# Gated linear attention followed by a ReGLU block: two tokens a partition in steps 0 and 1, one batch in each half of the partitions

## The chip, the cores and the metric

The kernel runs on one core of one Trainium2 chip. The metric is the device time of one execution in microseconds (us). Before the change it is 196.01 us, the median of three runs (194.18 to 196.87).

The engines go by the names of the profile: PE (TensorE, matmuls; PEld is its weight load), DVE (VectorE), ACT (ScalarE), POOL (GpSimd) and SP (SyncE, which here only issues DMAs). SPq and POOLq are the sequencers of SP and POOL at work on a DMA issue. L834 is line 834 of the kernel before.

## The reference

There are 4 batches, 8 heads, 768 tokens and a head dimension of 48. For each batch and head a state of 48 x 48 runs over the tokens, and its output goes through a feed-forward block with a ReLU gate:

```python
f = 1.0 / (1.0 + np.exp(-f_logit))
for t in range(S):
    state = f[:, :, t, :, None] * state + np.einsum('bhd,bhe->bhde', k[:, :, t], v[:, :, t])
    y[:, :, t] = np.einsum('bhd,bhde->bhe', q[:, :, t], state)
x = y.transpose(0, 2, 1, 3).reshape(B * S, H * D)       # 3072 x 384
out = (np.maximum(x @ w_gate, 0.0) * (x @ w_val)) @ w_out   # d_ff = 1536
```

## The kernel before, in words

**Tiling.** The 768 tokens are cut into six steps of C = 128 tokens. A step handles 128 tokens of all four batches; the batches go in two pairs (pair 0 is batches 0 and 1). Within a step the recurrence becomes matmuls. The logarithms of f are summed over the tokens by a matmul with a triangle of ones ("cum"). Their exponentials scale q and k to q-hat and k-hat ("hats"). Both are transposed, so that the head dimension lies in the partitions (qkT). Scores are k-hat times q-hat, masked to the triangle (ptm). x is scores times v plus q-hat times the old state. k-hat times v, added to the old state and scaled by the total decay, gives the new state. The feed-forward block follows: gate and val (L834, 12 slices of d_ff, three matmuls each), ReLU on ACT (L840), the product on DVE (L844), and the output matmuls (L877) with a copy on ACT (L887) and a store by SP (L891).

**Two ways for the attention.** Steps 1 to 5 have one token in each of the 128 partitions for f, k, q and v (`attention_front`, then `attention`): a load (L473) reads runs of 192 B, one for each token and head. Step 0 (`twos = (0,)`) has two tokens in a partition for f, k and q, so that its loads read runs of 384 B; its v is still loaded one token a partition. In step 0 partition 2r + b holds the tokens 2r and 2r + 1 of batch b of the pair. `attention_pair` computes the hats of a pair for both tokens i = 0 and 1, transposes them (L609) and copies k's transposes on DVE (L617) and q's on ACT (L616). `tokens` reads a batch's tokens from there in their natural order with a stride of two. Scores, rows and state of step 0 then run in `attention`, as in other steps. For step 0's state k-hat must stand with one token a partition, so `attention_back` transposes it back (L631, 4 matmuls a batch) and copies it on DVE (L636).

**Two ways for the transposes of the hats.** For (step, pair) in `pe_hats`, which are both pairs of steps 1 and 2, PE transposes (L694, 8 matmuls a batch) and DVE copies (L699). In steps 3 to 5 SP issues a transposing DMA, "the crossbar" (L702).

**Two ways for x.** "tiled" (steps 0 to 2): matmuls with 32 columns of weights, four tiles side by side in the array (L759), give x already transposed, which ACT copies to xT (L788). "xbar" (steps 3 to 5): full matmuls give x untransposed (L767, L771), ACT copies it (L793) and SP transposes it by DMA (L795).

**Scores** (L724) have 48 rows a head: even heads lie in the partitions from 0, odd ones from 64, and two run in the two halves of the array's rows. `s_twin` and `y_twin` name the pairs whose two batches' scores or rows are issued as one block.

**What sets the order.** The kernel contains a planner (`Plan`). Each instruction is added with an estimated time, a priority and the tiles that it reads and writes; a list scheduler with PSUM bank limits fixes the order of each engine's instructions and the semaphore waits. The order is then static: an engine that meets something that is not ready stands still, and all behind it waits. Loads go on SP's queue in the order of `first` and then step by step, at most `flight = 3` ahead; SP also issues the stores and the crossbar transposes, in one order. The weights (wg, wv, wo) are loaded by POOL's queue in three slices each; their issue waits for certain loads (`wg0@f0.1` means that wg's slice 0 waits until f of step 0, pair 1 has landed).

**The start.** While nothing else is ready, PE runs matmuls of zeros (L938).

Of the kernel before, what the change touches and what calls it, by code (L numbers as in the profile page):

```python
# [299 lines left out]
def bass_hgrn2_outer__then__ffn_reglu_kernel(  # L300
# [10 lines left out]
    twos = (0,)  # L311
    pe_hats = {(1, 0), (1, 1), (2, 0), (2, 1)}
    halves = {0: 6, 1: 6, 2: 6}
    x_way = {(c, pr): "tiled" if c < 3 else "xbar" for c in range(6) for pr in range(2)}
    s_twin = {(c, pr) for c in range(6) for pr in range(2)} - {(0, 0), (1, 0)}
    y_twin = {(1, 1), (2, 0), (2, 1)}
# [5 lines left out]
    C = 128  # L322
# [51 lines left out]
    pick2 = sb("pick2", [128, 2], BF16)  # L374
    ident = sb("ident", [128, 128], BF16)
# [4 lines left out]
    pl = Plan({"bc": 2, "bc4": 4, "tp": 2, "s": 4, "y": 2, "kv": 1, "f": 4})  # L380
# [28 lines left out]
    def triangle(t, name, base, prio):  # L409
# [9 lines left out]
                                         pattern=[[0, 64], [1, 2]], channel_multiplier=-1), ["pick"], ["pick"], occ=0.3, prio=-20)  # L419
# [10 lines left out]
    add("DVE", lambda: ve.tensor_copy(pick2[:], same.ap[:, 0:2]), [same], ["pick2"], occ=0.1, prio=-19)  # L430
# [30 lines left out]
    def load(n, c, b0, b1, after=()):  # L461
        last = tails.get("load")
        t = ld[n]
        both = c in twos and n != "v"
        if both:
            src = bass.AP(tensor=srcs[n].tensor, offset=b0 * H * S * D + c * C * D,
                          ap=[[2 * D, C // 2], [S * D, 2 * H], [1, 2 * D]])
            dst = bass.AP(tensor=t, offset=slot_of(n, c, b0 // 2) * 2 * HD, ap=[[NL[n] * 2 * HD, 128], [2 * D, H], [1, 2 * D]])
        else:
            src = bass.AP(tensor=srcs[n].tensor, offset=b0 * H * S * D + c * C * D,  # L470
                          ap=[[D, C], [S * D, (b1 - b0) * H], [1, D]])
            dst = t[:, slot_of(n, c, b0 // 2), :, :, :].rearrange("p b h d -> p (b h) d")
        op = add("SP", lambda: sy.dma_start(dst, src), [], in_keys(n, c, b0, b1),  # L473
                 occ=0.7 if both else 1.0, lat=0.9, prio=c * 100, after=after,
                 follows=[last] if last else [])
        tails["load"] = op
        dma(op, f"{n}{slot_of(n, c, b0 // 2)}", 0.95 * (b1 - b0), (64, 19, 27) if both else (128, 13.5, 23))
        return op
# [20 lines left out]
    loads, done = [], {}  # L499
    for item in first:  # L500
        item, _, behind = item.partition("@")
        gate = [done[behind]] if behind else []
        if item[0] == "w":
            op = load_w(item[:2], int(item[2:]), gate)
        else:
            c, pr = (int(x) for x in item[1:].split("."))
            op = load(item[0], c, 2 * pr, 2 * pr + 2, gate)
        done[item] = op
        if item[0] != "w":
            loads.append(op)  # L510

    def chain(line, *args, **kw):

        last = tails.get(line)
        tails[line] = add(*args, follows=[last] if last else [], **kw)
        return tails[line]
# [10 lines left out]
    def tokens(c, b, x, p, lo=0, hi=128):  # L527
        qi = (c * B + b) % NQ
        if c not in twos:
            return qkT[lo:hi, qi, x, p, :]  # L530
        row, two = NQ * 2 * NP * C, b % 2
        return bass.AP(tensor=qkT, offset=lo * row + (qi - two) * 2 * NP * C + x * 2 * NP * C + p * 2 * C + two,
                       ap=[[row, hi - lo], [2, C]])
# [18 lines left out]
    def attention_pair(c, b0):  # L552
# [3 lines left out]
        raw = {n: ld[n][:, slot_of(n, c, pr), :, :, :].rearrange("p b h d -> p (b h d)") for n in "fkq"}  # L556
        by_i = {n: raw[n].rearrange("p (h i d) -> p i h d", h=H, i=2) for n in "fkq"}
        key = {n: in_keys(n, c, b0, b0 + 2) for n in "fkq"}
# [6 lines left out]
            follows=tails.pop("first q", []), **act_t(2 * HD))  # L565
        heads = lambda b_: b_.ap[:, 0:HD].rearrange("p (h d) -> p h d", h=H)
        for i in range(2):
            bc, ek = Bank("bc4"), Bank("bc4")

            def cum(i=i, bc=bc):  # L570
                for o in range(2):
# [3 lines left out]
            ex = expo[:, e0 + i, 0, :]  # L575
            add("ACT", lambda bc=bc, ek=ek: sc.activation(ek.ap[:, 0:HD], bc.ap[:, 0:HD], AF.Exp, scale=1.0),
                [bc], [ek], prio=P + 2 + i, opens=[ek], **act_t(HD))
            eqk = bc if i else f"expq{e0}_0"
            add("ACT", lambda bc=bc, i=i, ex=ex: sc.activation(bc.ap[:, 0:HD] if i else ex, bc.ap[:, 0:HD], AF.Exp, scale=-1.0),
                [bc], [eqk], prio=P + 2 + i, **act_t(HD))  # L580
            e, hi = ("DVE" if i else "POOL"), his[i]
            hk_op = add("DVE", lambda i=i, hi=hi, ek=ek: ve.tensor_tensor(hats[:, hi, 1, :, 0:D], by_i["k"][:, i], heads(ek), ALU.mult),
                        key["k"] + [ek, f"hats{hi}"], hk_(hi), prio=P + 2 + i, **dve_t(HD))
            add(e, lambda e=e, i=i, hi=hi, bc=bc, ex=ex: engine[e].tensor_tensor(
                hats[:, hi, 0, :, 0:D], by_i["q"][:, i], heads(bc) if i else ex.rearrange("p (h d) -> p h d", h=H), ALU.mult),
                key["q"] + [eqk, f"hats{hi}"], hq_(hi), prio=P + 3 + i, follows=[hk_op] if i else [], **elem_t(e, HD))
# [9 lines left out]
        for j in range(2):  # L596
# [4 lines left out]
                [tot, f"dec{ai}"], [f"dec{ai}_{b}{j}{hh}" for b in (b0, b0 + 1) for hh in range(2)], prio=P + 10, **act_t(8))  # L601
        for x in (1, 0):
            tp = Bank("tp")

            def transposes(x=x, tp=tp):
                t16 = tp.ap[:, :].bitcast(BF16)
                for p in range(NP):
                    for i in range(2):
                        mm = te.transpose(t16[:, 2 * C * p:2 * C * (p + 1)].rearrange("q (r i b) -> q r i b", i=2, b=2)[:, :, i, :],  # L609
                                          hats[:, his[i], x, 2 * p:2 * p + 2, :].rearrange("p h d -> p (h d)"), ident[:])  # L610
# [4 lines left out]
            e = "DVE" if x else "ACT"  # L615
            op = add(e, (lambda tp=tp, dst=dst: sc.activation(dst, tp.ap[:, :].bitcast(BF16), AF.Copy)) if e == "ACT"  # L616
# [3 lines left out]
            if not x and b0 == 0:  # L620
                tails["first q"] = [op]

    def attention_back(c, b, behind):
        w = c * B + b
        hi, qi = w % NH, w % NQ
        tp = Bank("tp")

        def transposes():
            t16 = tp.ap[:, :].bitcast(BF16)
            for p in range(NP):  # L630
                mm = te.transpose(t16[:, p * C:(p + 1) * C], tokens(c, b, 1, p), ident[:])  # L631
            return mm
        P = w * 10
        tails["transposes"] = add("PE", transposes, ["ident", f"qkT{qi}_10", f"qkT{qi}_11"], [tp], occ=0.3, lat=PE_L, prio=P + 30,
                                  opens=[tp], follows=[behind, tails["transposes"]])
        add("DVE", lambda: ve.tensor_copy(hats[:, hi, 1, :, :].rearrange("p h d -> p (h d)"), tp.ap[:, :].bitcast(BF16)[:, 0:4 * C]),  # L636
            [tp], hk_(hi), prio=P + 31, follows=[behind], **dve_t(256))

    def attention_front(c, b):
# [32 lines left out]
        if c < NC - 1:  # L672
            for j in range(2):
# [9 lines left out]
        add("POOL", lambda: gp.tensor_tensor(hq, qin[:, b % 2, :, :], ex[:, 0, :].rearrange("p (h d) -> p h d", h=H),  # L683
                                             ALU.mult),
            in_keys("q", c, b, b + 1) + [f"expq{ei // 2 * 2}_{ei % 2}", f"hats{hi}"], hq_(hi), prio=P + 2, **pool_t(HD))
# [21 lines left out]
    def attention(c, bs):  # L707
        units = []
        for b in bs:
# [5 lines left out]
                in_keys("v", c, b, b + 1) + [f"vpad{w % NV}"], [f"v_{w % NV}"], prio=w * 10 + (55 if c in twos else 3), **pool_c(HD))  # L715
# [58 lines left out]
        xi, ybank, yop = c % NX, {}, {}  # L774
        tiled = x_way[c, bs[0] // 2] == "tiled"
        for part in ([units] if tiled and (c, bs[0] // 2) in y_twin else [[u] for u in units]):
# [4 lines left out]
            op = chain("intra", "PE", rows, [t for u in part for t in need(u) + ([f"vpad{u[1] % NV}"] if tiled else [])], ys,  # L781
                       occ=(0.34 if c else 0.19) * len(part) + 0.235 if tiled else 0.38, lat=PE_L, prio=part[0][1] * 10 + 7, opens=ys)
            for u, y in zip(part, ys):
                ybank[u[0]], yop[u[0]] = y, op
        for b, w, _ in units:
# [12 lines left out]
            if c in twos:  # L798
                behind.append(yop[b])
                later.append(lambda b=b, w=w: update(c, b, w))  # L800
            elif c < NC - 1:
                update(c, b, w)

    def update(c, b, w):
# [9 lines left out]
        if c in twos:  # L814
            attention_back(c, b, behind[-1])
        chain("state", "PE", state, hk_(hi) + [f"hats{hi}", f"v_{w % NV}"], [kv],
              occ=0.18, lat=PE_L, prio=P + (32 if c in twos else 6), opens=[kv])
        new_state(kv, c, b, w, P + (25 if c in twos else 0))
# [50 lines left out]
    def ffn_out(g, bs, cuts=1):  # L869
# [14 lines left out]
        for b in bs:  # L884
# [5 lines left out]
            both = [(bass.AP(tensor=out.tensor, offset=at, ap=[[DM, C], [1, DM]]), osb[oi][:, :])]  # L890
# [4 lines left out]
    groups = {c: [(0, 2, range(0, n)), (2, 4, range(0, n)), (0, 4, range(n, NJ))] for c, n in halves.items()}  # L895
    pend = []
    for c in range(NC):
# [4 lines left out]
        behind, later = [], []  # L902
        for b in range(0, B, 2):
# [5 lines left out]
            attention(c, (b, b + 1))  # L909
# [24 lines left out]
    order = pl.settle([(bk, warm_until if bk is spare else 0.0) for bk in banks], rounds=8, early=set(done.values()))  # L934
# [94 lines left out]
```

## Time and profile before

| | us |
|---|---|
| median of three runs | 196.01 |
| the profiled execution's own time | 195.26 |
| its span, first to last instruction | 193.5 |
| gate and val matmuls L834 (524 of 540 records) | 119.8 busy |
| output matmuls L877 | 49.5 busy |
| first L834 matmul starts | 16.58 |
| first store is issued | 46.44 |
| stores of step 1 are issued | 82.64 to 93.25 |

Busy times of PE overlap, since matmuls are pipelined and their ends are modelled; the chain, which counts each moment once, gives L834 36% and L877 23% of the span. The granted clock of TensorE is 1.000 over the span. "DMA share" in the stretches is the mean busy share of the core's 16 DMA engines; it passes 1 since an engine's packets overlap. Of the DMA packets, 86,016 have 192 B (loads of one token a partition), 6,144 have 384 B (f, k and q of step 0), 2,944 have 1536 B (stores) and 16,896 have 256 B (crossbar).

### The profile page before, as it was taken

The page shows a single profiled execution, that of the slowest core. Times are in us where ns is not written, and L with a number is a line of the kernel's source. Part 1 is how long each engine was busy: PE and PEld are TensorE (multiplying, and loading weights), DVE is VectorE, ACT ScalarE, POOL GpSimd, SP SyncE. Part 2 cuts the span into 40 slices and gives each one's busy share as a digit, 9 for nine tenths or more (in the row PEclk, how much of TensorE's full clock was granted, in tenths as well). Part 3 has the DMA queues.
Part 4 walks back from the last instruction along what each step waited for, and adds up shares of the span by engine and source line. Part 5 has one row for each costly group of instructions (what it writes and reads, how often), then busy time and mean ns, then how long its engine had stood idle before and what let it go on. Part 6 is the DMA issues. An engine that isn't in the chain of part 4 may idle for free.

```text
span 193.5 us, 4448 instructions
## 1 busy us (share of the span) xinstructions
PE 184.2 (95%) x1773; PEld 110.7 (57%) x1790; DVE 106.1 (55%) x195; ACT 111.0 (57%) x250; POOL 75.9 (39%) x108
## 2 busy tenths in 40 slices
PE   6986898999999999999999999999999999999995
PEld 1445694465788556767755544554555555544564
DVE  7756884671668878354776643743635622443300
ACT  3777439763596779838757758377343544244322
POOL 8377002958275949783533471634230000000000
PEclk9999999999999999999999999999999999999999
DMA  4999999999898999999796998998954220111113
GB/s 131 276 283 207 206 201 207 207 199 239 199 244 167 202 201 192 231 193 247 161 192 132 194 207 172 221 226 170 204 87 106 64 61 0 41 41 44 41 43 119
DMA packets 118196, 31.74 MB, mean 164 GB/s; under 512 B 111136, under 2 KB 118176, under 8 KB 118176
## 3 DMA queue, kind: packets, MB, share of 16 engines
q1 hardware_dynamic: 114192, 27.93, 68.1%
q0 software_dynamic: 3984, 3.54, 11.4%
q8 instruction: 14, 0.23, 0.5%
q14 instruction: 6, 0.05, 0.1%
HBM read 25.95 MB, written 4.72 MB: 158 GB/s over the span
## 4 chain that ended last, share of the span: by engine, by line
PE 70%; DMA 16%; SPq 5%; ACT 2%; DVE 2%; POOL 2%; issue 1%
PE ps L834 36%; PE ps L877 23%; DMA q_in<-in_q_dram 6%; DMA wv<-in_moe_w_val_dram 5%; SPq L473 4%; DMA f_in<-in_f_logit_dram 3%; DMA v_in<-in_v_dram 3%; PE ps L724 2%; PE ps L658 2%; PE ps L694 2%; PE ps L759 1%; PE ps L810 1%; DVE ptm L734 1%; PE ps L857 1%; POOL hats L683 1%
## 5 line engine op out<-in xcount | busy, mean ns | idle before, releaser
L844 DVE TENSOR_TENSOR gT<-relu,ps 128x512 bf16<-128x512 bf16 (+1 forms) x90 | 51.2, 578 | 53.9 <-PE ps L834 38.8
L834 PE MATMUL ps<-xT,wv 128*128 128x512 bf16 (+1 forms) x263 | 60.2, 336 | 1.8 <-DMA wv<-in_moe_w_val_dram 1.3
L840 ACT ACTIVATE relu<-ps 128x512 bf16<-128x512 f32 (+1 forms) x90 | 45.3, 511 | 27.6 <-PE ps L834 27.0
L834 PE MATMUL ps<-xT,wg 128*128 128x512 bf16 (+1 forms) x261 | 59.6, 335 | 0.9 <-ACT relu L840 0.5
L877 PE MATMUL ps<-wo,gT 128*128 128x384 bf16 x276 | 49.5, 326 | 0.1
L877 PEld LDWEIGHTS ps<-wo,gT 128*128 128x128 bf16 x276 | 25.9, 98 | 17.2
L834 PEld LDWEIGHTS ps<-xT,wv 128*128 128x128 bf16 x270 | 24.6, 98 | 19.4 <-DMA wv<-in_moe_w_val_dram 1.7
L834 PEld LDWEIGHTS ps<-xT,wg 128*128 128x128 bf16 x270 | 25.2, 98 | 17.9 <-ACT relu L840 0.4
L734 DVE TENSOR_TENSOR ptm<-ps,tri 128x512 bf16<-128x512 f32 x48 | 30.5, 684 | 8.3 <-PE ps L724 8.2
L680 POOL TENSOR_TENSOR hats<-k_in,expo 128x384 bf16<-128x384 f32 x20 | 19.8, 1000 | 20.8 <-ACT expo L668 11.0
L887 ACT ACTIVATE osb<-ps 128x384 f32<-128x384 f32 x23 | 11.2, 489 | 26.1 <-PE ps L877 26.1
L683 POOL TENSOR_TENSOR hats<-q_in,expo 128x384 bf16<-128x384 f32 x20 | 19.8, 1000 | 6.5 <-DMA q_in<-in_q_dram 6.5
L549 POOL TENSOR_TENSOR st<-ssum,dec 128x384 bf16<-128x384 f32 x16 | 13.3, 830 | 15.7 <-DVE ssum L547 15.5
L649 ACT ACTIVATE f_in<-f_in 128x768 f32<-128x768 f32 x10 | 8.4, 843 | 12.1 <-DMA f_in<-in_f_logit_dram 12.1
L714 POOL CAST vpad<-v_in 128x384 bf16<-128x384 f32 x24 | 11.7, 505 | 3.2 <-DMA v_in<-in_v_dram 3.2
L547 DVE TENSOR_TENSOR ssum<-ps,st 128x384 f32<-128x384 f32 x16 | 8.8, 552 | 4.9 <-PE ps L810 4.9
L668 ACT ACTIVATE expo<-ps 128x384 f32<-128x384 f32 x20 | 9.9, 493 | 0.5 <-PE ps L661 0.3
L670 ACT ACTIVATE expo<-ps 128x384 f32<-128x384 f32 x20 | 9.9, 496 | 0.0
L699 DVE COPY qkT<-ps 128x1024 bf16<-128x1024 bf16 x8 | 5.5, 690 | 7.5 <-PE ps L694 7.4
L724 PEld LDWEIGHTS ps<-qkT 48*128 48x128 bf16 x192 | 5.4, 94 | 5.3 <-issue 1.9
L651 ACT ACTIVATE bneg<-f_in 128x768 bf16<-128x768 f32 x10 | 8.4, 836 | 0.0
L724 PE MATMUL ps<-qkT 48*128 48x128 bf16 x192 | 7.6, 217 | 0.6 <-ACT qkT L616 0.5
(76 smaller groups left out, 146.2 us busy)
## 6 DMA issues: line engine op xcount, KB each, us to landing
f_in<-in_f_logit_dram SPq DMA_DIRECT2D x12, 384.0 KB, 5.6
k_in<-in_k_dram SPq DMA_DIRECT2D x12, 384.0 KB, 4.9
q_in<-in_q_dram SPq DMA_DIRECT2D x12, 384.0 KB, 5.7
v_in<-in_v_dram SPq DMA_DIRECT2D x12, 384.0 KB, 5.3
out_dram<-osb SPq DMA_DIRECT2D x23, 192.0 KB, 2.4
wg<-in_moe_w_gate_dram POOLq DMA_DIRECT2D x3, 384.0 KB, 7.7
wv<-in_moe_w_val_dram POOLq DMA_DIRECT2D x3, 384.0 KB, 8.8
wo<-in_moe_w_out_dram POOLq DMA_DIRECT2D x3, 384.0 KB, 6.2
```

The costliest lines, as they stand in the source:

```text
L549: add("POOL", lambda: gp.tensor_tensor(t4(s_new), t4(tmp), rate, ALU.mult), [key] + dk, [f"S{b}_{c % 2}"], prio=P + 8, **pool_t(HD))
L668: add("ACT", lambda: sc.activation(ex[:, 1, :], bc.ap[:, 0:HD], AF.Exp, scale=1.0), [bc], [f"expk{ei}"], prio=P + 1, **act_t(HD))
L680: add("POOL", lambda: gp.tensor_tensor(hk, kin[:, b % 2, :, :], ex[:, 1, :].rearrange("p (h d) -> p h d", h=H), ALU.mult), in_keys("k", c, ...
L683: add("POOL", lambda: gp.tensor_tensor(hq, qin[:, b % 2, :, :], ex[:, 0, :].rearrange("p (h d) -> p h d", h=H), ALU.mult), in_keys("q", c, ...
L714: add("POOL", lambda vin=vin, vout=vout: gp.tensor_copy(vout, vin.rearrange("p (n j) d -> p n j d", j=2)), in_keys("v", c, b, b + 1) + [f" ...
L724: mm = te.matmul(s[j].ap[:, p * C:(p + 1) * C], tokens(c, b, 1, p, lo, lo + D), tokens(c, b, 0, p, lo, lo + D))
L734: add("DVE", lambda mi=mi, j=j, s=s: ve.tensor_tensor(ptm[mi][:, j, :, :], s.ap[:, :].rearrange("p (n t) -> p n t", n=NP), mask, ALU.mult) ...
L834: mm = te.matmul(bank.ap[:, 0:n], wt[:, kt, j * 128:(j + 1) * 128], xT[xi][:, kt, n0:n1], start=(kt == 0), stop=(kt == NK - 1))
L840: add("ACT", lambda: sc.activation(relu[ri][:, 0:n], gate.ap[:, 0:n], AF.Relu), [gate], [f"relu{ri}"], prio=P, **act_t(n))
L844: add("DVE", lambda: ve.tensor_tensor(gT[gi][:, j, n0:n1], relu[ri][:, 0:n], val.ap[:, 0:n], ALU.mult), [val, f"relu{ri}"], [f"gT{gi}_{j}_ ...
L877: mm = te.matmul(o[b].ap[:, 0:DM], gT[gi][:, j, b * C:(b + 1) * C], wo[:, j, :], start=(j == 0), stop=(j == NJ - 1))
L887: add("ACT", lambda b=b, oi=oi: sc.activation(osb[oi][:, :], o[b].ap[:, 0:DM], AF.Copy), [o[b]], [f"osb{oi}"], prio=P, **act_t(DM))
```

## The change

**Two tokens a partition in steps 0 and 1, for f, k, q and v.** Each batch of a pair has 64 partitions of its own: partition 64b + r holds the tokens 2r and 2r + 1 of batch b. A load is two DMAs, one for each batch, of 64 partitions and runs of 384 B.

```diff
-    twos = (0,)
-    pe_hats = {(1, 0), (1, 1), (2, 0), (2, 1)}
+    twos = (0, 1)
+    pe_hats = set()
-    x_way = {(c, pr): "tiled" if c < 3 else "xbar" for c in range(6) for pr in range(2)}
-    s_twin = {(c, pr) for c in range(6) for pr in range(2)} - {(0, 0), (1, 0)}
-    y_twin = {(1, 1), (2, 0), (2, 1)}
+    x_way = {(c, pr): "tiled" if c < 4 else "xbar" for c in range(6) for pr in range(2)}
+    s_twin = {(c, pr) for c in range(6) for pr in range(2)}
+    y_twin = {(2, 0), (2, 1), (3, 0), (3, 1)}
+    on_dve = {(1, 0, 0, 0), (1, 0, 0, 1)}
...
-        both = c in twos and n != "v"
+        both, one = c in twos, b1 - b0 == 1
         if both:
-            src = bass.AP(tensor=srcs[n].tensor, offset=b0 * H * S * D + c * C * D,
-                          ap=[[2 * D, C // 2], [S * D, 2 * H], [1, 2 * D]])
-            dst = bass.AP(tensor=t, offset=slot_of(n, c, b0 // 2) * 2 * HD, ap=[[NL[n] * 2 * HD, 128], [2 * D, H], [1, 2 * D]])
+            row = NL[n] * 2 * HD
+            moves = [(bass.AP(tensor=t, offset=64 * i * row + slot_of(n, c, b0 // 2) * 2 * HD, ap=[[row, 64], [2 * D, H], [1, 2 * D]]),
+                      bass.AP(tensor=srcs[n].tensor, offset=(b0 + i) * H * S * D + c * C * D,
+                              ap=[[2 * D, C // 2], [S * D, H], [1, 2 * D]])) for i in range(2)]
```

**Steps 0 and 1 stay in `attention_pair` to the end.** The masks for the two tokens are built from `upto` and `below` by three adds on POOL (mask2). Scores are 64 keys by 128 queries for each token i, pair of heads, head and batch, in one quarter of the array each. Rows multiply 64 partitions of v by ptm, 32 columns of weights at a time. The state adds up over i from k-hat as it stands, so that `attention_back` and L631 are gone. q's transposes are copied on DVE too. In step 1 q-hat of pair 0 is computed on DVE (`on_dve`), its other hats on POOL.

```diff
+        def scores(its):
+            for i in its:
+                for p in range(NP):
+                    for j in range(2):
+                        for b in range(2):
+                            mm = te.matmul(s[i][j].ap[64 * b:64 * b + 64, p * C:(p + 1) * C],
+                                           tokens(c, b0 + b, 1, p, 64 * j, 64 * j + D, i), tokens(c, b0 + b, 0, p, 64 * j, 64 * j + D))
...
+            for i in range(2):
+                for at, (n, p, col, j) in enumerate(todo):
+                    lo = 32 * (n % 4)
+                    for b in range(2):
+                        mm = te.matmul(y[b].ap[lo:lo + 32, n // 4 * C:(n // 4 + 1) * C],
+                                       vpad[vs[i]][64 * b:64 * b + 64, col:col + 32], ptm[ms[i]][64 * b:64 * b + 64, j, p, :],
+                                       start=(first and i == 0 and at < 4), stop=(i == 1 and at >= 12), skip_group_check=True)
...
+            def state():
+                for p in range(NP):
+                    for i in range(2):
+                        for b in range(2):
+                            mm = te.matmul(kv[b].ap[:, p * 96:(p + 1) * 96],
+                                           hats[64 * b:64 * b + 64, his[i], 1, 2 * p:2 * p + 2, :].rearrange("p h d -> p (h d)"),
+                                           bass.AP(tensor=vpad[vs[i]], offset=64 * b * VW + p * VSTEP, ap=[[VW, 64], [64, 2], [1, D]]),
+                                           start=(i == 0), stop=(i == 1), skip_group_check=True)
```

**The queries of steps 0 and 1 stand in the order (i, r).** So x, the hidden layer and the output rows do, and the store puts them back: partition 64i + r goes to token 2r + i.

```diff
-            both = [(bass.AP(tensor=out.tensor, offset=at, ap=[[DM, C], [1, DM]]), osb[oi][:, :])]
+            both = [(bass.AP(tensor=out.tensor, offset=at, ap=([[DM, 2], [2 * DM, 64]] if g in twos else [[DM, C]]) + [[1, DM]]),
+                     osb[oi][:, :])]
```

**Step 2's hats are transposed by the crossbar** (`pe_hats` is empty) instead of by PE and DVE: four more transposing DMAs on SP's queue.

**Step 3's x is computed in tiles** instead of being transposed by the crossbar: four transposing DMAs fewer.

Other edits leave switches that are empty in this version (`act_copies`, `dve_q`, `single`, loads of a single batch). The PSUM limit of "kv" goes from 1 to 2. The planner's estimated times for the changed loads, scores, rows and states are new ones.

## The prediction

> **What bounds the kernel now.** I read the page's shares and its chain first, then the chain in order of time, then the stretches with the DMA share, then the DMA issues.
>
> ```profile
> span 193.5 us, 4448 instructions
> ...
> PE 184.2 (95%) x1773; PEld 110.7 (57%) x1790; DVE 106.1 (55%) x195; ACT 111.0 (57%) x250; POOL 75.9 (39%) x108
> ...
> PE 70%; DMA 16%; SPq 5%; ACT 2%; DVE 2%; POOL 2%; issue 1%
> ...
> out_dram<-osb SPq DMA_DIRECT2D x23, 192.0 KB, 2.4
> ```
>
> From about 30 us to the end the chain is nearly all PE: the end moves with the sum of PE's work, plus each moment at which PE's fixed order meets something that is not there yet.
>
> ```profile
> 42.84 0.33 PE ps L724 x8
> ...
> 44.58 0.56 PE ps L759 x28
> ...
> 48.49 0.45 PE ps L694 x8
> ...
> 51.50 0.55 PE ps L724 x16
> ...
> 55.93 0.90 PE ps L759 x56
> ...
> 61.94 0.82 ACT bneg L651
> 62.81 0.34 PE ps L658
> 63.15 0.08 PE ps L661 x4
> ...
> 87.80 0.17 PE ps L767 x4
> 87.97 0.20 PE ps L771 x8
> ```
>
> These are prices of PE work (start, length, what). The row at 61.94 is a wait: PE stands until ACT has turned a freshly landed f into bneg. The timeline of ACT shows that it got that f from DMA at 60.91, so it was used as it landed. In the list of waits ACT's L649 waited for f in 9 of its 10 runs. Late loads have little slack.
>
> ```profile
> core 0: us, PE busy (x) PEld busy (x) DVE busy (x) ACT busy (x) POOL busy (x), PEclk, DMA share, GB/s
> 5.00:15.00 10.00, 8.67 (x90) 4.37 (x89) 6.55 (x12) 7.27 (x16) 5.57 (x8) 1.00 1.18 276
> 15.00:25.00 10.00, 7.97 (x131) 6.20 (x131) 7.43 (x17) 5.52 (x13) 3.07 (x5) 1.00 1.24 206
> 35.00:45.00 10.00, 9.84 (x138) 5.58 (x137) 7.55 (x13) 5.70 (x14) 7.74 (x11) 1.00 1.26 209
> 45.00:90.00 45.00, 44.72 (x608) 31.11 (x600) 28.67 (x55) 31.26 (x80) 30.35 (x39) 1.00 1.06 209
> 90.00:135.00 45.00, 44.12 (x364) 25.33 (x368) 24.58 (x41) 30.83 (x68) 19.93 (x25) 1.00 0.91 188
> 170.00:175.00 5.00, 4.95 (x27) 2.57 (x27) 2.06 (x3) 1.60 (x4) 0.00 (x0) 1.00 0.11 39
> ```
>
> The last two columns are the DMA engines' share and rate. A full load shows as 1.24 to 1.26; until 135 us little is free. Loads in runs of 384 B (5 to 15 us) move 276 GB/s, in runs of 192 B some 206. The last row holds one store of 192 KB and nothing else of size.
>
> **PE's work.** From the prices above. (a) Step 2's hats leave PE: 4 blocks of L694 by 0.45 = -1.8 us. (b) The 16 transposes back of step 0 (L631) go: 16 by 0.056 (0.45/8) = -0.9. (c) Step 3's x: 4 by (0.17 + 0.20) = 1.48 becomes 2 twins by 0.90: +0.3. (d) Step 1's cum: a batch costs 0.16 + 0.08 now, a pair 0.48; then 4 by 0.16 and 8 tiny ones by 0.02 = 0.80: +0.3 a pair, +0.6. (e) Scores, rows and states of steps 0 and 1 become more, smaller matmuls. x8 and x16 of L724 differ by 0.22, 27 ns each in half the array's rows; x28 and x56 of L759 by 0.34 to 0.37, 13 ns each with four tiles side by side. A full matmul of 128 columns costs 56, so tiles do run side by side, and I take it that quarter and eighth tiles do so too: 32 scores by 13, 64 rows by 7, 16 states by 20 ns cost a pair what it costs now. If they go no faster than today's rate each, a pair pays 16 x 27 + 32 x 13 + 8 x 42 ns = 1.2 more, the four pairs 4.7. I take +0.3 for changes of tile shape. Sum: -1.5 (from -1.8 to +2.9).
>
> The Trainium skill's page "TensorE: Matmul & The Clock Gate" (section "Wait — 56ns, not 53.3ns?") holds that matmuls never start closer than about 25 ns. By it 64 rows would cost 1.6 us a pair instead of 0.45, and the sum over four pairs would be 4.6 us longer; the 13 ns of L759 already contradict it, and the measurement decides.
>
> **The start.** v of step 0 in 384 B runs saves 393 KB by (1/206 - 1/276) = 0.5 us a load, two loads ahead of the weights. PE's timeline shows waits of 0.60 and 0.71 for wv at 18 and 22 us, and 0.53 for ACT's copy of qkT, which goes to DVE (0.69 for 1.01). Against that, each load is issued as two: 16 DMAs for 8; the shortest load issue of SP is 0.37, the first one 0.74. From the fifth on SP's issue is held by the transfers themselves (2.39 for one), which covers them; if that cover is gone, 8 by 0.37 = 3 us. I take -0.6 (from -1.3 to +3). POOL's three mask adds (about 1 us, its 1000 ns for 384 columns and less) fall in its idle 3.4 us before L584. Two q products of step 1 move from POOL (1.0) to DVE (0.55 each) and the qkT copies to DVE; DVE is idle for a third of the time (28.7 of 45 us busy) and loses step 2's four qkT copies (0.69 each), two of which stand near the 4 us of DVE work that the chain passes through at 65 us; so nothing.
>
> **Queues.** Step 2's four qkT transposes join SP, 1.3 us of issue each, landing after 3.2 to 6.0 us; four xT ones leave (1.25 each). SP waits in order for the hats, with loads of step 3 behind: the like waits of steps 3 to 5 are 8.0 and 1.4 us in all at L702, so up to a third of that, 3 us, and I take nothing, as PE was seldom late for it. In DMA time the packets of 256 B (18 ns each) make 64 an engine for qkT, 24 for xT: 4 x (1.15 - 0.43) = +2.9 us. Step 1's eight loads and two v: 10 by 128 x 15 ns = 1.9 against 64 x 22 = 1.4: -5.1.
>
> **The stores, which decide.** x of steps 0 and 1 now stands in the order (i, r), so L891's destination becomes [2][64] rows where it was [128]. Every transfer of this trace has 64 or 128 as its outermost count on both sides; none shows how an outermost count of 2 is dealt out to the engines. Bounds: as today, each of 16 engines pays 0.11 x 5 us = 0.55 us (last row), no change; or two engines carry all, 0.55 x 8 = 4.4 each; a gain is excluded, since the bytes and the packets are the same. With the even split over the outermost count that fits all rows there are only two parts to deal, so I take the second. Eight stores, 8 x (4.4 - 0.55) = +30.8 us on two engines, and each load needs all 16. With the queues' terms: 30.8 + 2.9 - 5.1 = 28.6. What is free on them from 45 to 135 us is 45 x (1.26 - 1.06) + 45 x (1.26 - 0.91) = 24.8. If all of that took up the excess, loads would end (28.6 - 24.8)/1.26 = 3 us late, if none 23. Most of the free share lies after 90 us, where SP waits in order for results that would come late too: I take half, 13 us. f had no slack at 62 us, so PE stands that long in all.
>
> The Trainium skill's page "DMA: Bandwidth & Descriptors" (section "Rules for kernel authors") says that an outermost dimension smaller than 16 confines a transfer to at most that many engines. No run here shows it yet; by it the term would be the 30.8 us above, by an even deal over 16 nothing.
>
> **Sum.** Against the profiled execution (195.26 us, span 193.5): 195.3 - 1.5 - 0.6 + 13 = 206.2. The median of the runs shown, 196.01, is 0.75 higher; so 207.
>
> **The rivals.** (1) The stores stay spread over 16 engines. For it: nothing in the trace shows otherwise, and DMA then does less than before. Then 195.3 - 2.1 = 193.2, on the median 194. With the low ends of both terms it is 192.2, and 191 if PE's idle of 45 - 44.72 + 45 - 44.12 = 1.2 us goes too; with the high ends 195.3 + 2.9 + 3 = 201. It decides from the point where a store of steps 0 and 1 still lands in about 2.4 us. This is the case that ends not slower. (2) Two engines carry them, but the loads run ahead enough: 3 us late, 195.3 - 2.1 + 3 = 196.2, median 197. For it: step 1's loads end 4 us sooner; against it: the wait at 62 us. (3) The stores are harmless but the small tiles go at today's rate and SP's waits for step 2's hats cost their 3 us: 195.3 + 2.9 - 0.6 + 3 = 200.6, median 201. Against it: 13 ns a matmul.
>
> **Chances.** Forecast 0.62 (a lateness of 7 to 23 us gives 201 to 217 on the median), (1) 0.20, (2) 0.12, (3) 0.06. The range for 8 in 10 goes from 193 to 216: it leaves out the lower half of (1) and the top of the forecast. The forecast's own range is 201 to 216. A difference of 2%, 3.9 us, is about what can be told from none. Faster by more (below 192.1): a third of (1), 0.07. Within: the rest of (1), (2), and a third of (3): 0.27. Slower (over 199.9): the forecast and the rest of (3), 0.66.
>
> **What will show it.** Right: out_dram's stores of steps 0 and 1 land 4 us or more later than the 2.4 now; PE waits after 45 us for f, k, q, or v behind them, DMA's share falls while loads are late. Wrong: these stores land as before and PE stays at 4.9 of 5 us. PE's terms show as L694 with 32 matmuls fewer, no L631, and pairs of rows at about 0.9 us in step 1; the start as the first L834 before 16.6 us and the waits for wv.

## The result, and the profile after

The changed kernel takes 222.87 us (median of four runs, 221.62 to 224.66), where the kernel before takes 196.44 in the runs beside it. The ratio is 1.140, with a 95% interval of 1.126 to 1.153. The span of the profiled execution is 222.9 us, of before's 193.5: 29.4 more.

From the page of the changed kernel: the shares, three rows of the 40 slices (5.6 us each), the chain by engine, and the stores.

```profile
span 222.9 us, 4940 instructions
...
PE 191.2 (86%) x2014; PEld 113.7 (51%) x2031; DVE 107.6 (48%) x191; ACT 108.8 (49%) x244; POOL 74.7 (34%) x109
...
PE   7866999889977059994993599999999999999995
...
PEclk9995699999999659998599599999999999999999
DMA  5999999988643999999589999997799512000012
...
PE 55%; DMA 27%; SPq 11%; ACT 3%; issue 2%; POOL 2%
...
out_dram<-osb SPq DMA_DIRECT2D x23, 192.0 KB
```

PE has holes at about 75, 103 and 122 us, where before it had none. Beside and after each hole the granted clock falls, and ahead of the first the DMA share falls to 0.4 and 0.3. PE's share of the chain went from 70% to 55%, DMA's and SP's from 21% to 38%. The stores, which had a landing time of 2.4 us, have none that the page could work out.

PE's timeline of the changed kernel after 70 us (start, length, what, idle time before it and its releaser) gives the three longest waits:

```profile
80.55 1.03 PE L813 MATMUL ps<-qkT 48*128 48x128 bf16 x16 [9.45 <-DMA qkT<-hats]
...
105.50 1.03 PE L813 MATMUL ps<-qkT 48*128 48x128 bf16 x16 [3.24 <-DMA qkT<-hats]
...
124.99 1.03 PE L813 MATMUL ps<-qkT 48*128 48x128 bf16 x16 [6.13 <-DMA qkT<-hats]
```

These are 18.8 us, all for crossbar transposes of hats. The same 16 score matmuls take 0.55 us in undisturbed stretches and 1.03 here: after these waits PE starts at half its clock (the granted clock is 0.50 from 80.55 to 82 us).

SP's timeline of the changed kernel (start, length of the issue, what) shows what stood ahead of the first of them:

```profile
56.24 5.51 SPq L976 DMA_DIRECT2D out_dram<-osb  x1
61.79 0.68 SPq L485 DMA_DIRECT2D k_in<-in_k_dram  x1
62.51 6.10 SPq L791 DMA_TRANSPOSE qkT<-hats  x1
68.66 1.09 SPq L976 DMA_DIRECT2D out_dram<-osb  x2
69.80 5.99 SPq L791 DMA_TRANSPOSE qkT<-hats  x1
75.83 0.58 SPq L485 DMA_DIRECT2D q_in<-in_q_dram  x1
```

And the chain in order of time, of the changed kernel:

```profile
69.59 0.16 SPq L976
69.75 0.04 issue
69.80 10.51 DMA qkT<-hats
80.31 0.25 issue
80.55 1.03 PE ps L813 x16
...
105.03 7.81 DMA v_in<-in_v_dram
...
115.69 9.26 DMA qkT<-hats
```

Two stores are issued at 68.66. The transpose behind them is issued at 69.80 and lands 10.51 us later. The packets of the trace say why. The 256 packets of 1536 B of these two stores run from 70.09 to 78.82 us. From 75.1 to 78.7 us no other packet starts on any engine. Then 555 packets of 256 B, a quarter of those of the two transposes issued at 62.51 and 69.80, run from 78.78 to 79.73, and the transpose lands at 80.31. Issuing is held up as well: SP stands 5.51 us in one store and 6.10 in one transpose, where the longest were 2.03 and 2.86 before.

Here is one store's whole run of 128 such packets, from the first packet's start to the last one's end:

| | outermost count | one store, us |
|---|---|---|
| before, step 1 | 128 | 0.7 to 0.9 |
| after, steps 0 and 1 | 2 | 4.0 to 5.4 |

A single packet takes 65 ns in the middle (the median over all stores) in both kernels. The times of a store's packets, added up and divided by its run, tell how many are under way at once: 12.2 to 15.0 before (step 1), 2.1 after. So the work is the same, and it is done by two engines: 64 packets by 65 ns are 4.2 us. The trace does not name the engines; the two are inferred from these numbers.

The stretches of the changed kernel (the last three columns are clock, DMA share and GB/s):

```profile
45.00:60.00 15.00, 14.36 (x326) 9.44 (x316) 8.28 (x14) 7.58 (x20) 9.59 (x12) 1.00 0.84 169
60.00:80.00 20.00, 9.70 (x87) 7.35 (x86) 6.00 (x15) 8.02 (x23) 4.28 (x6) 0.84 0.63 88
...
105.00:125.00 20.00, 13.32 (x147) 9.03 (x148) 7.23 (x15) 6.01 (x14) 4.52 (x6) 0.76 0.83 120
```

The same stretch of the kernel before:

```profile
60.00:80.00 20.00, 19.79 (x289) 12.68 (x290) 15.29 (x29) 15.82 (x39) 13.93 (x19) 1.00 1.00 190
```

From 60 to 80 us PE is busy for 9.70 of 20 us, and the DMA engines move 88 GB/s where they moved 190. A mean share of 0.63 looks like free DMA capacity. It isn't of use: two engines carry the stores, and the transposes behind them end only when these two are done.

### The profile page after: what moved, and what is told of

Its sections match the earlier page's. It is cut to its first block, busy times and chain, and to the rows that moved or that the text cites. A ratio compares the mean times of both kernels' runs of the same rounds, so it can differ in the third digit from the quotient of the medians.

```text
span 222.9 us, 4940 instructions
## 1 busy us (share of the span) xinstructions
PE 191.2 (86%) x2014; PEld 113.7 (51%) x2031; DVE 107.6 (48%) x191; ACT 108.8 (49%) x244; POOL 74.7 (34%) x109
## 4 chain that ended last, share of the span: by engine, by line
PE 55%; DMA 27%; SPq 11%; ACT 3%; issue 2%; POOL 2%
PE ps L918 30%; PE ps L961 16%; DMA qkT<-hats 9%; SPq L485 8%; DMA q_in<-in_q_dram 7%; DMA wv<-in_moe_w_val_dram 4%; DMA v_in<-in_v_dram 4%; DMA f_in<-in_f_logit_dram 4%; PE ps L813 2%; SPq L976 2%; PE ps L747 1%; PE ps L848 1%; PE ps L941 1%; POOL hats L606 1%; PE ps L860 1%
## 5 line engine op out<-in xcount | busy, mean ns | idle before, releaser
L918 PE MATMUL ps<-xT,wv 128*128 128x512 bf16 (+1 forms) x266 | 62.9, 346 | 2.4 <-ACT relu L924 1.2
L918 PE MATMUL ps<-xT,wg 128*128 128x512 bf16 (+1 forms) x258 | 61.8, 348 | 1.2 <-ACT xT L704 0.5
L961 PE MATMUL ps<-wo,gT 128*128 128x384 bf16 x276 | 51.1, 334 | 0.0
L918 PEld LDWEIGHTS ps<-xT,wv 128*128 128x128 bf16 x270 | 26.2, 101 | 21.8 <-ACT relu L924 1.5
L961 PEld LDWEIGHTS ps<-wo,gT 128*128 128x128 bf16 x276 | 26.9, 100 | 18.8 <-issue 1.7
L918 PEld LDWEIGHTS ps<-xT,wg 128*128 128x128 bf16 x270 | 25.9, 101 | 19.4 <-issue 1.6
L823 DVE TENSOR_TENSOR ptm<-ps,tri 128x512 bf16<-128x512 f32 x32 | 20.2, 683 | 23.4 <-PE ps L813 23.4
L769 POOL TENSOR_TENSOR hats<-k_in,expo 128x384 bf16<-128x384 f32 x16 | 15.8, 998 | 31.7 <-ACT expo L757 18.5
L813 PE MATMUL ps<-qkT 48*128 48x128 bf16 x128 | 6.2, 251 | 18.8 <-DMA qkT<-hats 18.8
L773 POOL TENSOR_TENSOR hats<-q_in,expo 128x384 bf16<-128x384 f32 x16 | 15.7, 998 | 19.0 <-DMA q_in<-in_q_dram 19.0
L757 ACT ACTIVATE expo<-ps 128x384 f32<-128x384 f32 x16 | 7.9, 492 | 9.6 <-PE ps L750 9.5
L667 DVE TENSOR_TENSOR ptm<-ps,mask 128x512 bf16<-128x512 f32 x16 | 9.9, 683 | 1.1 <-PE ps L658 1.0
L803 POOL CAST vpad<-v_in 128x384 bf16<-128x384 f32 x16 | 7.8, 507 | 4.3 <-DMA v_in<-in_v_dram 4.3
L738 ACT ACTIVATE f_in<-f_in 128x768 f32<-128x768 f32 x8 | 6.7, 843 | 4.4 <-DMA f_in<-in_f_logit_dram 4.4
L759 ACT ACTIVATE expo<-ps 128x384 f32<-128x384 f32 x16 | 7.9, 491 | 0.0
```

The costliest lines, as they stand in the source:

```text
L667: add("DVE", lambda i=i, j=j, mask=mask: ve.tensor_tensor(ptm[ms[i]][:, j, :, :], s[i][j].ap[:, :].rearrange("p (n t) -> p n t", n=NP), ma ...
L769: add("POOL", lambda: gp.tensor_tensor(hk, kin[:, b % 2, :, :], ex[:, 1, :].rearrange("p (h d) -> p h d", h=H), ALU.mult), in_keys("k", c, ...
L773: add(e, lambda: engine[e].tensor_tensor(hq, qin[:, b % 2, :, :], ex[:, 0, :].rearrange("p (h d) -> p h d", h=H), ALU.mult), in_keys("q", ...
L813: mm = te.matmul(s[j].ap[:, p * C:(p + 1) * C], tokens(c, b, 1, p, lo, lo + D), tokens(c, b, 0, p, lo, lo + D))
L823: add("DVE", lambda mi=mi, j=j, s=s: ve.tensor_tensor(ptm[mi][:, j, :, :], s.ap[:, :].rearrange("p (n t) -> p n t", n=NP), mask, ALU.mult) ...
L918: mm = te.matmul(bank.ap[:, 0:n], wt[:, kt, j * 128:(j + 1) * 128], xT[xi][:, kt, n0:n1], start=(kt == 0), stop=(kt == NK - 1))
```

## The experiments

Medians of the kernel before were 196.5, 196.7, 197.4, 195.1 and 196.3 us beside the five groups of runs, so ratios are compared as well. Runs 2, 3 and 4 are of two executions each, the others of four or ten.

**1. After, with each store of steps 0 and 1 as two DMAs of 64 partitions.** Outermost count 64 in place of 2, the rest as it was.

```diff
-            both = [(bass.AP(tensor=out.tensor, offset=at, ap=([[DM, 2], [2 * DM, 64]] if g in twos else [[DM, C]]) + [[1, DM]]),
-                     osb[oi][:, :])]
+            if g in twos:
+                both = [(bass.AP(tensor=out.tensor, offset=at + i * DM, ap=[[2 * DM, 64], [1, DM]]), osb[oi][64 * i:64 * i + 64, :])
+                        for i in range(2)]
```

> Theory 1 (the stores of steps 0 and 1 run on two DMA engines; crossbar transposes and loads queue behind them, PE stands and its clock falls): with each of these eight stores cut into two DMAs of 64 partitions with rows of stride 2, packets spread over all engines again, the span of one store's packets falls from 4 to 5 us to under 1.5 us. PE's waits of 9.45, 3.24 and 6.13 us for qkT go and with them some 6 us at a lowered clock: 196 to 201 us. Rival (step 2's crossbar itself, or SP's order, makes the waits, the stores only stand beside them): above 215 us, the waits at 70, 102 and 118 us stay.

Measured: 202.78 us, ratio 1.034 (1.025 to 1.042), a little over the 196 to 201 expected. The edit takes 222.87 - 202.78 = 20.1 of the 26.4 us away. PE's waits and the stores in the profile of this run (vpad is v as POOL copies it for the matmuls):

```profile
PE ps L896 <- POOL vpad L803: 1.9, 1, 1.9
...
PE ps L813 <- DMA qkT<-hats: 1.1, 3, 0.7
```

```profile
out_dram<-osb SPq DMA_DIRECT2D x16, 96.0 KB, 3.0
```

The waits for qkT fell from 18.8 to 1.1 us, and the halves land after 3.0 us. The packets of a store's two halves take 0.8 to 2.9 us, not always the 1.5 expected. The spans differ by 222.9 - 200.6 = 22.3 us. PE's idle time between its first and its last matmul falls from 28.1 to 9.9 us (18.2) and its busy time from 191.2 to 187.1 (4.1); these are the 22.3. So about a fifth of what the stores cost here is slower matmuls (mean clock 0.923 against 0.974), and the rest is waiting.

**2. Before, with only the stores of steps 0 and 1 dealt as [2][64].**

```diff
-            both = [(bass.AP(tensor=out.tensor, offset=at, ap=[[DM, C], [1, DM]]), osb[oi][:, :])]
+            both = [(bass.AP(tensor=out.tensor, offset=at, ap=([[DM, 2], [2 * DM, 64]] if g < 2 else [[DM, C]]) + [[1, DM]]), osb[oi][:, :])]
```

> The kernel before, only its stores of steps 0 and 1 get the destination [2][64] rows (the output rows of these two steps then stand in another order). Theory 1: eight stores of 4 us and more on two engines, PE waits behind them, 206 to 220 us. Rival: a store that is off the chain costs nothing, 195 to 198 us.

Measured: 222.28 us, ratio 1.133 (1.124 to 1.142), a little over the 206 to 220 expected: one edit in an access pattern makes the kernel before as slow as the changed one. It costs about 26 us alone (0.133 x 196), more than the 20.1 of run 1. Against the profile before, PE is idle for 16.8 us more and busy for 10.0 us more, at a mean clock of 0.946. PE's waits in this run:

```profile
PE ps L810 <- POOL vpad L714: 7.3, 1, 7.3
PE ps L724 <- DMA qkT<-hats: 4.3, 1, 4.3
PE ps L694 <- POOL hats L683: 4.2, 1, 4.2
PE ps L834 <- ACT relu L840: 3.2, 1, 3.2
```

The waits go by other names than in the changed kernel. What comes late is what stands behind a store on SP's queue: here v, f and a transpose (the chain holds an f that lands 10.57 us after its issue), there mostly transposes.

**3. Before, with the stores dealt as [4][32].** The like edit with four parts.

> The kernel before with the destination of the stores of steps 0 and 1 as [4][32] rows (output rows of these steps in another order). Theory 1 (as many engines as the outermost count): one store's packets take about 32 x 65 ns = 2.1 us instead of 4.2 in e2 and 0.6 in the kernel before; the time lies between, 200 to 212 us. Rival (any destination that is not plain rows of 128 goes to two engines): as e2, 222 us.

Measured: 209.31 us, ratio 1.070 (1.048 to 1.091), between the two. In the trace a store of step 1 takes 2.5 to 4.0 us in packets, against 4.3 to 5.4 with two parts in run 2 and 0.7 to 0.9 with 128; 3.4 to 3.9 of its packets are under way at once. Twice the parts, half the loss: 13 us in place of 26.

The Trainium skill's page "DMA: Bandwidth & Descriptors", in "Rules for kernel authors", has an outermost dimension smaller than 16 confine a transfer to at most that many engines. The runs with two and four parts agree (about 2 and almost 4 packets at once).

**4. After, with step 2's hats on PE again** (`pe_hats = {(2, 0), (2, 1)}`).

> The changed kernel with the hats of step 2 transposed on PE again. Theory 1: the long wait at 70 us for qkT goes, but loads behind the stores are late as well, and step 3's crossbar stays: 205 to 218 us. Rival (the crossbar in step 2 is the cause): 198 us or less.

Measured: 225.67 us, ratio 1.150 (1.141 to 1.159). This misses the 205 to 218 expected: the time does not fall when step 2 leaves the crossbar. PE then waits 9.9 us for later transposes and 6.3 for vpad.

**5. Run 1, with each load of steps 0 and 1 as one DMA of 128 partitions.** About 6 us were left in run 1, and it begins its feed-forward matmuls late.

```diff
-            moves = [(bass.AP(tensor=t, offset=64 * i * row + slot_of(n, c, b0 // 2) * 2 * HD, ap=[[row, 64], [2 * D, H], [1, 2 * D]]),
...
+            src = bass.AP(tensor=srcs[n].tensor, offset=b0 * H * S * D + c * C * D,
+                          ap=[[2 * D, C // 2], [S * D, 2 * H], [1, 2 * D]])
+            dst = bass.AP(tensor=t, offset=slot_of(n, c, b0 // 2) * 2 * HD, ap=[[NL[n] * 2 * HD, 128], [2 * D, H], [1, 2 * D]])
```

> The stores as in e1, and each load of steps 0 and 1 is one DMA of 128 partitions as in the kernel before (partition 2r + b instead of 64b + r, so the tokens stand in other partitions than the matmuls assume; same bytes, same runs). Theory: the start is late because SP issues 16 DMAs of 0.65 us where it issued 8, and the DMA engines wait for the issue: f of pair 1 lands at 10.4 instead of 11.8 us, the first gate matmul starts 2 to 3 us earlier, the time is 2.5 to 3.5 us below e1. Rival (the start is late for another reason, such as the 64 partitions or the masks): within 1 us of e1.

Measured: 199.66 us, ratio 1.013 (1.001 to 1.025): 3.1 us less than run 1. That is the number of the theory; whether its reason, SP's issue, holds is what run 7 asks.

**6. Run 1, with ten more matmuls of zeros in the start**, seven ahead of pair 1's cum and three ahead of pair 0's rows.

> e1 with ten more matmuls of zeros on PE, seven ahead of the cum of pair 1 (PE stood 1.8 us there in e1) and three ahead of the rows of pair 0. Theory: the late loads leave PE idle between 11 and 16 us, the granted clock falls (0.83 from 16.6 to 35 us), and that costs 2 to 3 us; here the clock stays near 1.0 in that stretch and the time is 1.5 to 3 us below e1. Rival: the stretch waits for data anyway, the clock costs nothing: within 1 us of e1.

Measured: 202.70 us, ratio 1.034: no gain. Two stretches from 15 to 25 us, of this run and then of run 1:

```profile
15.00:25.00 10.00, 6.72 (x158) 4.84 (x156) 6.85 (x13) 4.05 (x12) 5.02 (x7) 1.00 1.25 210
```

```profile
15.00:25.00 10.00, 8.19 (x161) 6.11 (x159) 5.95 (x12) 3.83 (x11) 5.01 (x7) 0.66 1.23 205
```

The clock is full where it was 0.66, and PE does about the same matmuls (158 and 161) in 1.5 us less busy time, and then waits that much longer. In this stretch the DMA engines are full (1.25) and PE waits for what they bring, so the low clock there cost nothing that shows in the time.

**7. Run 1, with the second halves of step 0's loads of pair 0 issued by ACT.**

```diff
+        mine = moves[:1] if both and c == 0 and b0 == 0 else moves
+            for op, d, s_ in by_act:
+                sc.dma_start(d, s_).then_inc(op.sem, 16)
```

> e1 with the second half of each of the four loads of step 0, pair 0 issued by ACT, which is idle then, instead of SP. Theory (SP's issue of 0.65 us for each half is the limit at the start): SP is 2.6 us earlier with pair 1's loads, f of pair 1 lands 1.5 to 2.5 us earlier, the time is 1.5 to 3 us below e1. Rival (halves of 64 partitions are slow by themselves): within 1 us of e1.

Measured: 202.87 us, ratio 1.039 (1.026 to 1.052): no gain either. ACT starts on f of pair 1 at 11.48 us instead of 12.62, but the packets of 384 B still took 29 ns in the middle. SP's issue of twice as many DMAs is not what makes halves slow.

**8. Run 1, with step 2's hats on PE again.**

> e1 with step 2's hats transposed on PE and DVE again. Theory: with the stores mended the crossbar of step 2 costs more in waits (0.7 us for qkT, 1.9 us for vpad behind it on SP's queue, and a lower clock after them) than the 1.8 us of PE work that it saves: 0.5 to 2.5 us below e1. Rival: the 1.8 us of PE work come back, 1 to 2 us above e1.

Measured: 204.24 us, ratio 1.045 (1.033 to 1.057). That is 1.5 us above run 1, within both intervals; in any case no gain.

**9. Before, with step 3's x in tiles** (`c < 4` in `x_way`, and (3, 0), (3, 1) in `y_twin`).

> The kernel before with one part of the change alone: x of step 3 in tiles. By the prediction's terms +0.3 us of PE and four crossbar transposes fewer on SP's queue: 195 to 197.5 us. Rival (the tiles' rows wait for the old state and cost more than the crossbar did): 199 us or more.

Measured: 196.56 us, ratio 0.999 (0.995 to 1.004). This part is worth nothing either way.

**10. Before, with step 2's hats on the crossbar** (`pe_hats = {(1, 0), (1, 1)}`).

> The kernel before with another part alone: step 2's hats over the crossbar. By the prediction's terms -1.8 us of PE, waits of 0 to 3 us on SP's queue: 194 to 198 us. Rival (the long landing of 3 to 6 us stops PE's fixed order in each of the four blocks): 200 us or more.

Measured: 202.24 us, ratio 1.024 (1.012 to 1.036). The chain of this run in order of time:

```profile
66.79 4.37 DMA v_in<-in_v_dram
71.16 0.05 issue
71.21 0.97 POOL vpad L714 x2
72.18 2.02 SPq L702
...
76.22 6.48 DMA v_in<-in_v_dram
...
83.32 0.34 PE ps L810 x4
```

SP stands at L702 until the hats are there, the loads of v behind it are issued late, and vpad and the state matmuls (L810) follow. This is the wait that the prediction bounded at 3 us and then set to nothing. It costs about 4.7 us alone (0.0239 x 197.4).

**11. Run 1, with step 0 alone in the new manner** (`twos = (0,)`; step 1's hats on PE, step 2's on the crossbar).

> e1 with two tokens a partition in step 0 only; step 1 has one token a partition and its hats transposed on PE, as in the kernel before. If step 1's halves and its new order cost the rest: 198 to 200 us. If the rest is lost at the start (step 0): within 1.5 us of e1's 202.8.

Measured: 202.17 us, ratio 1.027 (1.016 to 1.038), as run 1. What is left does not come from step 1's new manner.

**12 and 13. Run 11 with step 2's hats on PE too, and then also with the loads as one DMA each.** Step 1's rows are issued batch by batch in both.

> The run in which only step 0 has two tokens a partition (stores as two transfers), and now step 2's hats go over TensorE as well, as in the kernel before: no hats go over the crossbar. Theory: the 6 us that are left beside the kernel before lie at the start and in the crossbar of step 2; alone on the kernel before the crossbar cost 4.6 us, so this run loses 3 to 5 us against step 0 alone (202.2): 197.5 to 199.5, ratio 1.00 to 1.015, with the step 0 copies ending 2 to 3 us later than the 53.0 of before and that lead kept. Rival (the planner's order gives back on PE what the crossbar frees, as it did when both steps were new): 201 to 204, ratio 1.02 to 1.04.

> The same, and the loads of step 0 as one transfer of 128 partitions each (tokens in other partitions, so the rows come in another order: only its time is read). Theory: halves of 64 partitions cost 2 to 3 us at the start: 194.5 to 197.5, ratio 0.99 to 1.005, within the uncertainty of the kernel before. Rival (the start is set by something else): as the run beside it, within 1 us.

Measured: 201.78 us, ratio 1.032 (1.027 to 1.038), and 198.65 us, ratio 1.018 (1.013 to 1.022). Run 12 went as its rival said: undoing the crossbar of step 2 gains nothing here, though it cost 4.7 us alone. Run 13 gives 3.1 us once more for whole loads, as run 5 did; here the two intervals do not touch. The first gate matmul starts at 16.60 us in run 13, as in the kernel before (16.58), and at 20.06 in run 12. The start in the stretches of run 12 and then of run 13:

```profile
5.00:10.00 5.00, 4.17 (x31) 1.98 (x30) 3.51 (x7) 3.67 (x8) 1.12 (x3) 1.00 1.23 235
10.00:15.00 5.00, 2.97 (x60) 1.85 (x57) 3.84 (x7) 2.26 (x4) 2.67 (x4) 1.00 1.29 233
```

```profile
5.00:10.00 5.00, 4.03 (x37) 2.21 (x36) 3.56 (x8) 3.44 (x9) 2.01 (x5) 1.00 1.15 318
10.00:15.00 5.00, 3.28 (x120) 2.08 (x119) 4.47 (x8) 3.54 (x8) 4.07 (x6) 1.00 1.16 250
```

In both kernels the engines are full (a share of 1.15 to 1.29), but the halves move 235 GB/s and the whole loads 318. A packet of 384 B takes 31 ns in the middle in run 12 and 22 in run 13. PE does 60 matmuls between 10 and 15 us with halves, 120 with whole loads.

**14. Run 13, with step 3's x and step 1's twins as before.** Of the change, step 0 is left: its attention, its v in runs of 384 B and its stores as two DMAs, and with it the planner's new limit and estimates.

> As the last run (two tokens a partition in step 0 alone, each of its loads as one transfer, step 2's hats over TensorE; tokens in other partitions, so only its time is read), and now step 3's x over the crossbar and the twins of step 1 as in the kernel before. What is left new is step 0's attention alone. Theory: the 3.6 us still left lie in step 0's new manner and its planner order, since step 3's x was neutral alone: 198 to 199.5, ratio 1.01 to 1.02. Rival (they come from step 3's x or step 1's rows, in this order of instructions): 195 to 197, ratio 0.995 to 1.007.

Measured: 198.88 us, ratio 1.012 (1.007 to 1.017). So about 2.3 us (0.012 x 196) of what is left after the stores and the halves come with these. The time of step 0 itself is not it: the last copy of step 0's output starts at 52.3 us, where it was 53.0 before. Step 1's last one starts at 92.3 (91.2), step 2's at 135.0 (131.0). The loss comes afterwards, in steps whose work is unchanged but is planned in another order. Among PE's waits there are:

```profile
PE ps L896 <- POOL vpad L803: 2.2, 2, 1.5
...
PE ps L783 <- POOL hats L773: 1.0, 1, 1.0
```

That a change of order makes them is argued, not shown, and which one stays open. No run was faster than the kernel before; the one with step 3's x in tiles equals it.

## Why the prediction was wrong

It gave 207 us (193 to 216), and 222.87 was measured. The direction and the mechanism were right: stores on two engines, and PE waiting for what is issued behind them. The size was wrong, in the main term above all.

- **The stores on two engines: right.** 4.4 us for a store was forecast from 0.55 x 8, and 4.0 to 5.4 were measured. Run 2 shows that this edit alone makes the loss, and run 3 that it goes with the number of parts.
- **"I take half, 13 us": the step that failed.** The term was put at 13 us, and it is 20.1 in the changed kernel (run 1). That lies within its bounds of 3 and 23, but the prediction shows no row from which the half could be read. On the kernel before, the same stores cost about 26 us alone (run 2), more than the upper bound, which is 30.8/1.26 = 24.4 without the queues' terms. Two things are shown that the half did not count. SP's issues were themselves held, for up to 5.51 and 6.10 us (in run 2 two loads for 7.75 and 8.05), and what stood behind came later still. And a PE that waits 3 to 9 us starts again at half its clock: 4.1 us of run 1's gain are less busy time of PE, and run 2 has 10.0 us more of it than the kernel before. How the miss divides between the two is not shown. With the term, PE's work and the start all at their upper bounds the sum would have been 195.3 + 2.9 + 3 + 23 + 0.75 = 225; the range stopped at 216.
- **The free DMA time was hardly of use.** The 24.8 us from 45 to 135 us were free on every engine of the kernel before, on the two as well. Of the excess of 30.8 us 20.1 came through all the same, and in run 2 about 26. In the stretch from 60 to 80 us of the changed kernel the mean share is 0.63: a load of q is issued at 75.83 us, and its first packet starts at 79.46, though from 75.1 to 78.7 only the stores' packets start.
- **PE's work: -1.5 forecast, -0.3 to -0.9 found.** Summed from start to start, with each gap cut off at 0.2 or at 0.3 us, PE's matmuls outside the feed-forward block take 36.6 or 37.7 us before and 36.3 or 36.9 in run 1. The small tiles do run side by side: 64 rows take 0.67 us a pair, 10.5 ns each, 32 scores 0.57 and 16 states 0.44. The forecast's prices (0.45, 0.42 and 0.32) were a third to a half too low. The cum's +0.6 came out (0.85 us a pair for 0.52), and so did the transposes back. Today's rate for each tile, on which rival 3 rested, is refuted: 64 rows would have taken 0.83. So are the 1.6 us that the prediction works out for them beside it.
- **The start: -0.6 forecast, 2 to 3.4 us of loss found**, near the upper bound of +3 but for another reason. The first L918 starts at 19.65 us where the first L834 did at 16.58; the first matmul of 512 columns comes at 33.68 instead of 30.27. The bound was worked out from SP's issue time. Run 7 shows that the issue is not it, and runs 5 and 13 that whole loads bring the start back (3.1 us in each pair of runs). The saving for v was reckoned at 276 GB/s, and halves reach 235.
- **Step 2's crossbar: "nothing" was wrong for the kernel before, and its bound of 3 us too low** (4.7 in run 10). In the changed kernel it can't be shown to cost anything (runs 8 and 12). Its cost depends on the rest of the kernel, so it can't be added to the other terms.
- **Step 3's x: +0.3 forecast, 0 measured** (run 9, 0.999).
- **DVE: "so nothing".** The two q products that moved were taken at 0.55 us each and took 1.81 (last section). No run prices this alone.
- **What the profile was to show.** Late stores (their last packets end 6 to 11 us after the issue), waits after 45 us and a falling DMA share are all there. The waits were said to be for f, k, q and v; the three largest are for qkT.

**The wait at 62 us was misread.** The prediction has PE stand at 61.94 until ACT is done with bneg. PE's timeline of the kernel before has matmuls there, and PE stands about 0.2 us:

```profile
62.26 0.49 PE L834 MATMUL ps<-xT,wg 128*128 128x256 bf16 x3
62.81 0.34 PE L658 MATMUL ps<-bneg,tri 128*128 128x384 bf16 x1
```

That f had no slack there is right all the same. "Nearly all PE" from 30 us on was too strong: of the 20.9 us of the chain from 92.86 to 113.79 only 1.8 are PE's, and 11.0 are loads of v and q.

Together: 20.1 (stores, run 1) + 3.1 (half loads, run 5) leave 26.4 - 23.2 = 3.2 us, of which about 2.3 come with step 0's new manner (run 14). The difference between these two is below what the runs can tell.

## What to carry to other kernels

Look at the outermost count of both access patterns of every DMA, of stores off the chain too. Here a permutation of rows turned 128 into [2][64], two engines did all the work (2.1 packets at once), and the transposes and loads issued behind them came late. Split such a store into DMAs with a long outermost count, but do not halve a load of 128 partitions without need. A low mean share of the DMA engines says nothing about the one that the transfers wait for. A forecast that has found such a bottleneck, and has no row for the share of it that comes through, should put its range at the bounds and not its sum at half.

## What the runs showed of the hardware that was not expected

**Half loads are slower for each packet.** The same 384 B took 22 ns in transfers of 128 partitions (before, run 13) and 28 to 31 in transfers of 64 (after and runs 1, 7 and 12), with the engines full in both. Run 7 rules out SP's issue; why a packet takes longer stays open.

**A product on DVE from SBUF beside POOL.** The groups of the changed kernel's DVE (operation, counts, then busy time and mean ns of one):

```profile
L606 DVE TENSOR_TENSOR hats<-q_in,expo 128x384 bf16<-128x384 f32 x2 | 3.5, 1806 | 0.0
...
L606 DVE TENSOR_TENSOR hats<-q_in,ps 128x384 bf16<-128x384 f32 x2 | 1.1, 548 | 0.0
```

The two q products of step 1 that moved from POOL to DVE have both operands in SBUF and took 1806 ns each. The second row has one operand in PSUM; from such products the 0.55 us had been taken. They ran from 36.42 to 39.96 us, while POOL worked without a break from 36.18 to 39.06.

The Trainium skill's page "SBUF — State Buffer", in "SBUF: two separate sides", says that a DVE operation with two inputs in SBUF and a GpSimd operation that reads SBUF hold a shared pair of ports in turn, each for its whole instruction. These two rows agree; no run here takes POOL's work away to prove it.

**The clock is not worth keeping up everywhere.** After waits of 3 to 9 us the scores took 1.03 instead of 0.55 us, and that is lost at the end. At the start, where PE waits for loads, full clock gained nothing (run 6: 202.70 us against 202.78).
